# A decayed linear attention and a two-layer network on one core: the first layers of the last two token groups by seven products

## The chip, the core and the metric

The kernel runs on one core of a Trainium2 chip. A core has a matrix engine (TensorE, PE in the profile; its weight loads are listed as PEld), a vector engine (VectorE, DVE), a scalar engine for activation functions (ScalarE, ACT), a general engine (GpSimd, POOL) and a queue engine that issues transfers (SyncE, SP). Each works through its own list of instructions in order and waits for the others by semaphores. TensorE writes its sums to PSUM, eight banks of 128 rows by 512 float32 numbers; VectorE and ScalarE read and write PSUM and the main on-chip memory, SBUF.

The metric is the time of one execution on the device, in microseconds (us), as a median over runs. The profile is of one further execution; its span runs from the first to the last instruction.

## The reference

```python
# q, k, v: (4, 8, 768, 64)   lam: (8,)   w_in: (512, 2048)   w_out: (2048, 512)
for b in range(768 // 64):                       # blocks of 64 positions, each with a running state
    intra = (qb @ kb.T * Dmask) @ vb             # Dmask[i, j] = lam ** (i - j) for i >= j, else 0
    inter = (qb * lam_pow) @ kv_state            # lam ** (i + 1)
    out[:, :, sl] = intra + inter
    kv_state = lam ** 64 * kv_state + (kb * rev_pow).T @ vb
x = out.transpose(0, 2, 1, 3).reshape(3072, 512) # 8 heads of 64 side by side
h = x @ w_in
g = h * tanh(softplus(h))                        # Mish
return g @ w_out                                 # (3072, 512) float32
```

## The kernel before, in words

**Groups.** The 768 positions are cut into six groups (`NG`) of 128 (`C`); a group holds the 128 positions of all four batches, so 512 tokens (`GT`). For each group there are three kinds of work. Attention, batch by batch: `scores` (L238; matmuls into banks e and o, masked by DVE into `sb`), `outputs` (L259; matmuls into bank z, scaled by DVE into `xn`, turned by a transfer of SP into `xt`, the group's tokens in the layout for the first layer), `state` (L286; bank e, then DVE and POOL). The first layer: `x @ w_in` with Mish. The second layer: the product with `w_out`.

**The first layer, plain.** A *unit* (`unit`, L322) is 128 of the 2048 hidden columns for all 512 tokens: four matmuls of 512 columns into one bank and one Mish on ACT into `hsg`. Group `n + 1` has units 0 to 15. The banks A, B and C take turns (`next_bank`, L329). The weights `w_in` lie in four tiles `win[0]` to `win[3]` of 512 hidden columns each, so four units read one tile.

**The second layer by seven products.** `dense2` (L427) uses the Strassen-Winograd scheme: the product is cut into 2 x 2 blocks, and seven block products of sums take the place of eight. It works on banks G and H, in 14 *halves*: product 1, 2, 6, 5, 7, 3, 4, each for two blocks of tokens; a half is eight matmuls of 256 columns. Product 1 is copied from G to H by ACT (L440) before product 2 is added to G; product 5 goes by ACT to SBUF (`r5`, L447) and DVE makes `u4` from it and H (L449) before product 7 is added to H. The sums of hidden values that the products read are made by DVE (`token_sum`, L369), those of the weights once (`weight_sum`, L356).

**The order of the work.** It is written out by hand; each engine's list has the order of the program text. The loop at L701 runs n = 1 to 4. In iteration n, TensorE does the first layer of group n + 1 (units, `u`), the second layer of group n (halves, `h`), and for n up to 3 the attention of group m = n + 2 (`s_` for scores, `o_` for outputs). These are interleaved so that a half or a unit lies between an operation on another engine and the matmul that waits for it. At the end of iterations 1 to 3 the first two halves of group n + 1 are done. In iteration 4 there is no attention left. In iteration 3 it is that of the last group, which needs no `state`. After the loop `dense2_alone` (L479) does the second layer of the last group.

**Transfers.** POOL issues the loads of q, k and v, SP the transposes of k and q (`turn_dma`, L227), of `xn` and the stores. `kT` and `qT` have three buffers, each of two batches of a group.

Of the kernel before, what the change touches and what calls it, by code (L numbers as in the profile page):

```python
# [7 lines left out]
F32 = mybir.dt.float32  # L8
F16 = mybir.dt.float16
AF = mybir.ActivationFunctionType  # L10
ALU = mybir.AluOpType
# [9 lines left out]
def kernel(  # L21
# [10 lines left out]
    nc = tc.nc  # L32
    B, H, S, D = q.shape
    C = 128
    NG = S // C
    JP = H // 2
# [8 lines left out]
    WS = 4  # L45
# [43 lines left out]
    win = [const.tile([128, NKC, WQ], F16, name=f"win{s}") for s in range(WS)]  # L89
# [108 lines left out]
    xt, kT, qT, kd, sb, wst = {}, {}, {}, {}, {}, {}  # L198
# [7 lines left out]
    def flat(t, j):  # L206
        return t[:, 2 * j : 2 * j + 2, :].rearrange("p h c -> p (h c)")

    turned = {}

    def turn_pe(n, b, banks):

        srcs = (kn[n, b], qn[n, b])
        for src, name, to, tag in zip(srcs, ("kT", "qT"), (kT, qT), banks):
            pt = bank(tag, [JP, C], F16)
            for j in range(JP):
                nc.tensor.matmul(pt[:, j, :], flat(src, j), ident, is_transpose=True,
                                 start=(j == 0), stop=(j == JP - 1))
            if b % 2 == 0:
                turned[name, n] = work.tile([128, 2 * JP, C], F16, name=name, tag=name, bufs=3)  # L220
            to[n, b] = turned[name, n][:, b % 2 * JP : b % 2 * JP + JP, :]
            if name == "kT" or n > 0:
                nc.scalar.activation(to[n, b], pt, AF.Copy)
            else:
                nc.vector.tensor_copy(to[n, b], pt)

    def turn_dma(n, bp):  # L227
        for t, to in (("k", kT), ("q", qT)):
            tile_ = work.tile([128, 2 * JP, C], F16, name=f"{t}T", tag=f"{t}T", bufs=3)
            nc.sync.dma_start_transpose(out=tile_, in_=pairs[t, n, bp].rearrange("p h c -> p (h c)"))  # L230
            for i in range(2):
                to[n, 2 * bp + i] = tile_[:, i * JP : (i + 1) * JP, :]
# [113 lines left out]

    class Set:
        pass

    tsum = [const.tile([128, HK, HN], F16, name=f"tsum{i}") for i in range(4)]  # L350

    def w_quarter(r, c, s):

        return wout[2 * r + s][:, :, c * HN : (c + 1) * HN]

    def weight_sum(i, s):  # L356

        ks = slice(s * NKI // WS, (s + 1) * NKI // WS)
        a, b, op = (
            (w_quarter(0, 1, s), w_quarter(0, 0, s), ALU.subtract),  # L360
            (w_quarter(1, 1, s), tsum[0][:, ks, :], ALU.subtract),
            (w_quarter(1, 1, s), w_quarter(0, 1, s), ALU.subtract),
            (w_quarter(1, 0, s), tsum[1][:, ks, :], ALU.subtract),
        )[i]
        nc.vector.tensor_tensor(out=tsum[i][:, ks, :], in0=a, in1=b, op=op)
# [52 lines left out]
    def product(n, p, t, blk, fresh, lo=0, hi=HN):  # L418
        lhs, rhs = operands(n, p)
        for kk in range(HK):  # L420
            nc.tensor.matmul(t, lhs(kk, blk), rhs(kk)[:, lo:hi], start=(fresh and kk == 0),  # L421
                             stop=(kk == HK - 1), skip_group_check=True)

    def osum():
        return work.tile([128, 2, HN], F32, name="osum", tag="osum", bufs=3)
# [53 lines left out]
    def dense2_alone(n):  # L479

        x, z = bank("G", [2, HN]), bank("H", [2, HN])
        y = [(bank("A", [HN]), 0, 0, HN), (bank("B", [HN // 2]), 1, 0, HN // 2),
             (bank("C", [HN // 2]), 1, HN // 2, HN)]
        keep = lambda name: work.tile([128, 2, HN], F32, name=name, tag=name, bufs=1)

        def both(p, t, fresh):
            for blk in range(2):
                product(n, p, t[:, blk, :], blk, fresh and blk == 0)

        both(1, x, True)  # L490
# [10 lines left out]
        u3, u2 = keep("u3"), keep("u2")  # L501
# [12 lines left out]
        for t, blk, lo, hi in y:  # L514
            product(n, 3, t, blk, False, lo, hi)
        for t, blk, lo, hi in y:
            o = osum()
            nc.vector.tensor_tensor(out=o[:, blk, lo:hi], in0=t, in1=u2[:, blk, lo:hi], op=ALU.add)
            store(n, 0, 1, o[:, blk : blk + 1, lo:hi], blk, lo, hi)
# [48 lines left out]
    def sums(n, part, *which):  # L568
        for i in which:
            token_sum(n, i, part)  # L570
# [61 lines left out]
    later[3]()  # L632
    two_units(1, 12, 0)
    turn_dma(2, 1)

    def attend(n, b, kd_eng):
# [56 lines left out]
    def h(m=1):  # L693
        for _ in range(m):
            halves.pop(0)()
# [2 lines left out]

    for n in range(1, NG - 1):  # L701
        m = n + 2
        last = m >= NG - 1

        def u(*units):
            for ni in units:
                unit(n + 1, ni, next_bank())

        def s_(b):
            if m < NG:  # L710
                if not last:
                    decay_k(m, b, nc.vector)
                scores(m, b)

        def o_(b):
            if m < NG:
                outputs(m, b)
                if not last:
                    state(m, b, "e", nc.gpsimd)

        def fetch(*what):
            if m + 1 < NG:
                for t, bp in what:
                    load_pair(t, m + 1, bp)

        s_(0)
        if m < NG:
            turn_dma(m, 1)
        u(0)
        sums(n, 1, 0, 1)  # L730
        if n == 1:
            weight_sum(3, 0)
            weight_sum(3, 1)
        h(1)
        u(1)
        h(1)
        u(2)
        o_(0)
        fetch(("k", 0), ("q", 0))
        u(3)  # L740

        h(1)
        u(8)
        s_(1)
        sums(n, 1, 2, 3)
        h(1)
        u(9, 10)
        o_(1)
        fetch(("v", 0), ("k", 1))
        h(1)  # L750
        u(11)

        h(1)
        u(4)
        s_(2)
        if m + 1 < NG:
            turn_dma(m + 1, 0)
        u(5)
        h(1)
        u(6)  # L760
        o_(2)
        fetch(("q", 1), ("v", 1))
        h(1)
        sums(n + 1, 0, 0, 1)
        h(1)
        u(7)

        s_(3)
        h(1)
        u(12)  # L770
        h(1)
        o_(3)
        u(13)
        sums(n + 1, 0, 2, 3)
        h(1)
        u(14)
        if n + 1 < NG - 1:
            halves = dense2(n + 1)
            h(1)
        u(15)  # L780
        if n + 1 < NG - 1:
            h(1)

    sums(NG - 1, 1, 2, 0, 1, 3)
    dense2_alone(NG - 1)


# [28 lines left out]
```

## Time and profile before

| | |
|---|---|
| median of three runs | 213.22 us (211.72 to 213.25) |
| the profiled execution | 213.27 us |
| its span | 211.3 us |
| mean granted TensorE clock | 0.996 |
| iteration n = 3 of the loop | 140.45 to 170.06, 29.6 us |
| iteration n = 4 | 170.06 to 194.39, 24.3 us |
| `dense2_alone` and the last stores | 194.39 to 211.30, 16.9 us |

A row of the timeline gives start, duration, engine, line, operation and its tiles (written <- read), and in brackets the engine's idle time before it with what ended it. A matmul row's duration includes an end that overlaps the next matmuls, so the distance from one row's start to the next one's is what a block of matmuls takes of TensorE. The chain of waits lists these distances directly. DVE and ACT rows can overlap their neighbours in the same way.

### The profile page before, as it was taken

What the parts mean: (1) busy time and instruction counts of PE and PEld (TensorE: products, weight loads), DVE (VectorE), ACT (ScalarE), POOL (GpSimd) and SP (SyncE); (2) the same over time, 40 slices, a digit from 0 to 9 for tenths busy, and PEclk for the clock granted to TensorE, in tenths of its full rate; (3) what the DMA queues carried; (4) which work ended last, traced back from release to release, by engine and by line L of the source; (5) the groups of instructions that cost most, each with busy time, mean ns of one, the idle gap of its engine ahead of it and who ended that gap; (6) DMA issues with size and microseconds to landing.
All of it is one profiled execution on the core that took longest, in us unless ns stands there. A gap on an engine that the chain in (4) does not pass through costs nothing.

```text
span 211.3 us, 4221 instructions
## 1 busy us (share of the span) xinstructions
PE 201.0 (95%) x1757; PEld 135.0 (64%) x1757; DVE 124.5 (59%) x202; ACT 88.1 (42%) x152; POOL 77.6 (37%) x75
## 2 busy tenths in 40 slices
PE   7798999899999999999999999999999999999991
PEld 2366545688765456667666667766667765666891
DVE  6738749872875857647965657953638340153341
ACT  5354676658531124342254342254342454525300
POOL 7999554524565760653530763410000000000020
PEclk9999999999999999999999999999999999999998
DMA  8999999999939999799992499991112401013033
GB/s 128 140 162 206 159 179 158 187 207 174 127 75 129 214 158 170 156 139 128 177 250 74 55 153 135 169 248 55 21 28 74 119 8 50 0 50 102 0 102 99
DMA packets 109365, 26.23 MB, mean 124 GB/s; under 512 B 99490, under 2 KB 108834, under 8 KB 109346
## 3 DMA queue, kind: packets, MB, share of 16 engines
q0 software_dynamic: 77600, 13.37, 81.1%
q1 hardware_dynamic: 30704, 12.33, 28.0%
q10 hardware_dynamic: 1042, 0.26, 0.6%
q8 instruction: 14, 0.23, 0.4%
q14 instruction: 5, 0.04, 0.1%
HBM read 27.26 MB, written 6.29 MB: 159 GB/s over the span
## 4 chain that ended last, share of the span: by engine, by line
PE 85%; DVE 3%; DMA 3%; POOL 3%; ACT 2%; issue 2%; ACTq 0%; DVEq 0%
PE bG L421 15%; PE bH L421 13%; PE bB L314 11%; PE bC L314 11%; PE bA L314 11%; PE be L243 4%; PE bB L340 2%; PE bz L263 2%; PE bz L268 2%; DMA q<-in_q_dram 2%; PE bA L340 2%; PE bG L472 2%; PE bC L340 2%; PE bC L472 2%; POOL kd L236 1%
## 5 line engine op out<-in xcount | busy, mean ns | idle before, releaser
L314 PEld LDWEIGHTS <-win 128*128 128x128 f16 x328 | 30.4, 98 | 23.7 <-issue 0.3
L298 POOL TENSOR_TENSOR w<-raw,lbm 128x512 f16<-128x512 f32 x14 | 20.0, 1428 | 52.1 <-DVE raw L297 52.1
L421 PEld LDWEIGHTS <-gsum 128*128 128x128 f16 x336 | 30.9, 98 | 7.3
L247 DVE TENSOR_TENSOR sb<-be,dm 128x512 f16<-128x512 f32 x24 | 16.5, 687 | 22.6 <-PE bo L243 22.5
L421 PEld LDWEIGHTS <-hsg 128*128 128x128 f16 x240 | 23.4, 98 | 7.8
L314 PE MATMUL bA<-xt,win 128*128 128x512 f16 (+2 forms) x112 | 27.9, 372 | 0.2
L314 PE MATMUL bC<-xt,win 128*128 128x512 f16 x108 | 27.7, 379 | 0.0
L320 ACT ACTIVATE hsg<-bA 128x512 f16<-128x512 f32 x27 | 16.1, 597 | 26.1 <-PE bA L314 26.1
L314 PE MATMUL bB<-xt,win 128*128 128x512 f16 (+2 forms) x108 | 26.9, 371 | 0.0
L271 DVE TENSOR_TENSOR xn<-bz,lq 128x512 f16<-128x512 f32 x20 | 13.8, 690 | 19.8 <-PE bz L268 19.8
L320 ACT ACTIVATE hsg<-bB 128x512 f16<-128x512 f32 x26 | 15.5, 598 | 23.6 <-PE bB L314 23.6
L503 POOL TENSOR_TENSOR u<-u,u 128x512 f32<-128x512 f32 x1 | 1.3, 1273 | 64.2 <-DVE u L502 64.2
L320 ACT ACTIVATE hsg<-bC 128x512 f16<-128x512 f32 x27 | 16.2, 598 | 20.3 <-PE bC L314 20.2
L421 PE MATMUL bH<-tsum,gsum 128*128 128x256 f16 x160 | 20.4, 273 | 0.0
L421 PE MATMUL bG<-wout,hsg 128*128 128x256 f16 x160 | 20.2, 273 | 0.0
L384 DVE TENSOR_TENSOR gsum<-hsg 128x1024 f16<-128x1024 f16 x20 | 15.0, 752 | 6.4 <-ACT hsg L320 6.4
L247 DVE TENSOR_TENSOR sb<-bo,dm 128x512 f16<-128x512 f32 x24 | 16.3, 679 | 0.0
L340 PEld LDWEIGHTS <-win 128*128 128x128 f16 x128 | 12.1, 98 | 2.2 <-issue 0.6
L84 POOL DMA_DIRECT2D kn<-in_k_dram x10 | 12.0, 1199 | 2.8 <-PE be L289 1.6
L449 DVE TENSOR_TENSOR u<-bH,r 128x512 f32<-128x512 f32 x4 | 2.8, 690 | 17.3 <-ACT r L447 17.3
L84 POOL DMA_DIRECT2D qn<-in_q_dram x10 | 11.9, 1186 | 1.4 <-PE bz L263 0.7
L84 POOL DMA_DIRECT2D vn<-in_v_dram x10 | 11.9, 1187 | 0.3 <-issue 0.2
(119 smaller groups left out, 306.9 us busy)
## 6 DMA issues: line engine op xcount, KB each, us to landing
out_dram<-osum SPq DMA_DIRECT2D x23, 256.0 KB, 2.6
kn<-in_k_dram POOLq DMA_DIRECT2D x10, 256.0 KB, 8.8
qn<-in_q_dram POOLq DMA_DIRECT2D x10, 256.0 KB, 6.9
vn<-in_v_dram POOLq DMA_DIRECT2D x10, 256.0 KB, 8.3
wout<-in_moe_w_out_dram POOLq DMA_DIRECT2D x4, 512.0 KB, 15.2
win<-in_moe_w_in_dram POOLq DMA_DIRECT2D x3, 512.0 KB, 9.5
vz<-in_v_dram POOLq DMA_DIRECT2D x4, 128.0 KB, 4.5
kn<-in_k_dram POOLq DMA_DIRECT2D x3, 128.0 KB, 4.5
```

What stands on the lines that cost most here:

```text
L84: nc.gpsimd.dma_start(out=tile_, in_=rows(src, n, 2 * bp, 2))
L243: nc.tensor.matmul(p_[t][:, j, :], kT[n, b][rs, j, :], qT[n, b][rs, j, :], start=True, stop=True)
L247: nc.vector.tensor_tensor(out=sb[n, b, t], in0=p_[t], in1=dm[:, t], op=ALU.mult)
L263: nc.tensor.matmul(po[:, 2 * j : 2 * j + 2, :].rearrange("p h e -> p (h e)"), qT[n, b][:, j, :], wst[n, b][:, j, :], start=(j == 0), stop= ...
L271: nc.vector.tensor_tensor(out=xn, in0=po, in1=bc(lq, 2, D), op=ALU.mult)
L298: eng.tensor_tensor(out=w_new, in0=raw, in1=lbm, op=ALU.mult)
L314: nc.tensor.matmul(open_[n, ni][:, lo:hi], win[ni // 4][:, kc, (ni % 4) * 128 : (ni % 4) * 128 + 128], xt[n][:, kc, lo:hi], start=(opens a ...
L320: nc.scalar.activation(h_tile(n)[:, ni, :], open_.pop((n, ni)), AF.Mish)
L340: nc.tensor.matmul(t[:, u, :], win[ni // 4][:, kc, m : m + 128], xt[n][:, kc, cs], start=(u == 0 and kc == 0), stop=(kc == NKC - 1), skip_ ...
L384: nc.vector.tensor_tensor(out=gsum[n, i][:, ks, :], in0=a, in1=b, op=op)
L421: nc.tensor.matmul(t, lhs(kk, blk), rhs(kk)[:, lo:hi], start=(fresh and kk == 0), stop=(kk == HK - 1), skip_group_check=True)
L472: nc.tensor.matmul(po, hsg[n][:, ki, b * C : (b + 1) * C], wout[part][:, kk, :], start=(ki == 0), stop=(ki == NKI - 1))
```

## The change

Iterations 1 and 2 keep units; iterations 3 and 4 (first layers of groups 4 and 5) use *sets*. A set is one tile `win[s]`: 512 hidden columns for 512 tokens, cut into 2 x 2 blocks of hidden columns and tokens and 2 of the inner dimension. Seven products of four matmuls of 256 columns (`seven`) replace sixteen matmuls of 512 columns. The sets come in the order s = 0, 2, 1, 3.

One set runs as follows, with three banks a, b, c: product P1 into a; ACT copies a to b (`seed`); P2 is added to a, and ACT's Mish reads it. P5 goes into c and ACT copies it to SBUF (`p5`). P6 is added to b; DVE writes b + p5 into c. P7 is added to b; DVE writes b + p5 to SBUF (`c22`). P3 is added to c, then Mish. Mish of `c22`, P4 added to b, Mish of b. P4 and the last two Mish are *owed*: they come after the next set's P1, scores and seed (`settle`), so the seed of a set stands ahead of them on ACT. In iteration 3 the banks are A, B, C and, for every other set, A, C, B; in iteration 4 A, B, C and e, z, o.

The products read sums of tokens (`x_sums`: four DVE operations of 512 float16 elements per row, at the start of iterations 3 and 4) and sums of weights (`w_sum`: four per set, kept in `wsum`). The weight sums of the four sets are made on DVE in iterations 1 and 2, two places in each, behind the token sums of `s_(1)` and behind unit 5.

Besides: `kT` and `qT` have two buffers instead of three; the transposes of group m + 1, batches 0 and 1, are issued ahead of unit 4 and `s_(2)` instead of behind them; `dense2_alone` uses the tiles `p5` and `c22` for its `u3` and `u2`.

```diff
-                turned[name, n] = work.tile([128, 2 * JP, C], F16, name=name, tag=name, bufs=3)
+                turned[name, n] = work.tile([128, 2 * JP, C], F16, name=name, tag=name, bufs=2)
...
+    def w_sum(s, i, eng):
+        w, t = win[s], wsum[s]
+        a, b_, op = (
+            (w[:, 0:2, HC:], w[:, 2:4, HC:], ALU.add),
+            (t[:, 0], w[:, 0:2, 0:HC], ALU.subtract),
+            (w[:, 0:2, 0:HC], w[:, 0:2, HC:], ALU.subtract),
+            (w[:, 2:4, 0:HC], t[:, 1], ALU.subtract),
+        )[i]
+        eng.tensor_tensor(out=t[:, i], in0=a, in1=b_, op=op)
...
+    def x_sums(n):
+        x = xt[n]
+        t = [work.tile([128, 2, HC], F16, name=f"xsum{i}", tag=f"xsum{i}", bufs=1) for i in range(4)]
+        xsum[n] = t
+        for i, (a, b_) in enumerate((
+            (x[:, 0:2, HC:], x[:, 0:2, 0:HC]),
+            (x[:, 2:4, HC:], t[0]),
+            (x[:, 2:4, HC:], x[:, 0:2, HC:]),
+            (x[:, 2:4, 0:HC], t[1]),
+        )):
+            nc.vector.tensor_tensor(out=t[i], in0=a, in1=b_, op=ALU.subtract)
...
+    def seven(o, i, t, fresh):
+        w, x, ws, xs = win[o.s], xt[o.n], wsum[o.s], xsum.get(o.n)
+        for u in range(2):
+            for kk in range(2):
+                us = slice(u * 128, u * 128 + 128)
+                lhs, rhs = (
+                    lambda: (w[:, kk, us], x[:, kk, 0:HC]),
+                    lambda: (w[:, 2 + kk, us], x[:, 2 + kk, 0:HC]),
+                    lambda: (ws[:, 3, kk, us], x[:, 2 + kk, HC:]),
+                    lambda: (w[:, 2 + kk, HC + u * 128 : HC + u * 128 + 128], xs[3][:, kk, :]),
+                    lambda: (ws[:, 0, kk, us], xs[0][:, kk, :]),
+                    lambda: (ws[:, 1, kk, us], xs[1][:, kk, :]),
+                    lambda: (ws[:, 2, kk, us], xs[2][:, kk, :]),
+                )[i - 1]()
+                nc.tensor.matmul(t[:, u, :], lhs, rhs, start=(fresh and u == 0 and kk == 0),
+                                 stop=(kk == 1), skip_group_check=True)
...
+    def set_step(o, step):
+        if step == "m1":
+            o.a = bank(o.banks[0], [2, HC])
+            seven(o, 1, o.a, True)
+        elif step == "seed":
+            o.b = bank(o.banks[1], [2, HC])
+            nc.scalar.activation(o.b, o.a, AF.Copy)
+        elif step == "m2":
+            seven(o, 2, o.a, False)
+            mish(o, 0, 0, o.a)
+        elif step == "m5":
+            o.c = bank(o.banks[2], [2, HC])
+            seven(o, 5, o.c, True)
+            o.p5 = work.tile([128, 2, HC], F32, name="p5", tag="p5", bufs=1)
+            nc.scalar.activation(o.p5, o.c, AF.Copy)
+        elif step == "m6":
+            seven(o, 6, o.b, False)
+            nc.vector.tensor_tensor(out=o.c, in0=o.b, in1=o.p5, op=ALU.add)
+        elif step == "m7":
+            seven(o, 7, o.b, False)
+            o.c22 = work.tile([128, 2, HC], F32, name="c22", tag="c22", bufs=1)
+            nc.vector.tensor_tensor(out=o.c22, in0=o.b, in1=o.p5, op=ALU.add)
+        elif step == "m3":
+            seven(o, 3, o.c, False)
+            mish(o, 0, 1, o.c)
+        elif step == "m4":
+            mish(o, 1, 1, o.c22)
+            seven(o, 4, o.b, False)
+            mish(o, 1, 0, o.b)
...
+    KINDS = {1: "pppp", 2: "pppp", 3: "ssss", 4: "ssss"}
+    WSUMS = {(1, 0): (0,), (1, 1): (2,), (2, 0): (1,), (2, 1): (3,)}
...
+        for i, x in enumerate((0, 2, 1, 3)):
+            alone = (("A", "B", "C"), ("e", "z", "o")) if m >= NG else (("A", "B", "C"), ("A", "C", "B"))
+            turn = i % 2 if kinds[i - 1] == "s" else 0
+            sets.append(set_of(n + 1, x, alone[turn]) if kinds[i] == "s" else None)
+        owed = []
...
+        def settle():
+            while owed:
+                mm(owed.pop(), "m4")
+        def opening(i):
+            if kinds[i] == "s":
+                mm(i, "m1")
+                s_(i)
+                mm(i, "seed")
+                settle()
+            elif i == 0:
+                s_(i)
+        def closing(i):
+            mm(i, "m7", "m3")
+            owed.append(i)
...
+        opening(0)
         if m < NG:
             turn_dma(m, 1)
+        if "s" in kinds:
+            x_sums(n + 1)
+        if kinds[0] == "s":
+            h(1)
+            mm(0, "m2", "m5")
+            sums(n, 1, 0, 1)
+            h(1)
+            mm(0, "m6")
+            o_(0)
+            fetch(("k", 0), ("q", 0))
+            closing(0)
...
+        opening(1)
         h(1)
+        if kinds[1] == "s":
+            mm(1, "m2", "m5")
+            sums(n, 1, 2, 3)
+            h(1)
+            mm(1, "m6")
+            o_(1)
+            fetch(("v", 0), ("k", 1))
+            h(1)
+            closing(1)
...
+        opening(2)
         h(1)
         if m + 1 < NG:
             turn_dma(m + 1, 0)
+        if kinds[2] == "s":
+            mm(2, "m2", "m5", "m6")
+            o_(2)
+            fetch(("q", 1), ("v", 1))
+            h(1)
+            closing(2)
+            h(1)
+            sums(n + 1, 0, 0, 1)
+            h(1)
...
+        opening(3)
+        if kinds[3] == "s":
+            h(1)
+            mm(3, "m2", "m5")
+            h(1)
+            mm(3, "m6")
+            o_(3)
+            h(1)
+            mm(3, "m7", "m3")
+            owed.append(3)
+            sums(n + 1, 0, 2, 3)
...
+        more = n + 1 < NG - 1
+        if more:
             halves = dense2(n + 1)
             h(1)
+        settle()
+        if kinds[3] != "s":
+            u(15)
+        if more:
             h(1)
```

More of the change, by code (lines that the diff above doesn't have):

```diff
@@ new lines, in set_of @@
+    def set_of(n, s, banks):
+        o = Set()
+        o.n, o.s, o.banks = n, s, banks
+        return o
+    def seven(o, i, t, fresh):
[14 more added lines that the diff above has]
+                                 stop=(kk == 1), skip_group_check=True)
@@ L500, in dense2_alone @@
         both(6, z, False)
-        u3, u2 = keep("u3"), keep("u2")
+        u3, u2 = keep("p5"), keep("c22")
         nc.vector.tensor_tensor(out=u3, in0=z, in1=p1, op=ALU.add)
@@ L724, in fetch, with ws @@
                     load_pair(t, m + 1, bp)
-        s_(0)
+        def ws(n, i):
+            for x in WSUMS.get((n, i), ()):
+                for t in range(4):
+                    w_sum(x, t, nc.vector)
+        kinds = KINDS[n]
+        sets = []
+        for i, x in enumerate((0, 2, 1, 3)):
+            alone = (("A", "B", "C"), ("e", "z", "o")) if m >= NG else (("A", "B", "C"), ("A", "C", "B"))
+            turn = i % 2 if kinds[i - 1] == "s" else 0
+            sets.append(set_of(n + 1, x, alone[turn]) if kinds[i] == "s" else None)
@@ new lines, with mm @@
+        owed = []
+        def mm(i, *steps):
+            for x in steps:
+                set_step(sets[i], x)
+        def settle():
[12 more added lines that the diff above has]
+            owed.append(i)
@@ L754 @@
-        u(4)
-        s_(2)
+        if "s" in kinds:
[9 more added lines that the diff above has]
+            closing(0)
+        else:
+            u(0)
+            sums(n, 1, 0, 1)
+            if n == 1:
+                weight_sum(3, 0)
+                weight_sum(3, 1)
+            h(1)
+            u(1)
+            h(1)
+            u(2)
+            o_(0)
+            fetch(("k", 0), ("q", 0))
+            u(3)
@@ new lines @@
+        opening(1)
+        h(1)
+        if kinds[1] == "s":
[7 more added lines that the diff above has]
+            closing(1)
+        else:
+            u(8)
+            settle()
+            s_(1)
+            sums(n, 1, 2, 3)
+            ws(n, 0)
+            h(1)
+            u(9, 10)
+            o_(1)
+            fetch(("v", 0), ("k", 1))
+            h(1)
+            u(11)
@@ L756 @@
+        opening(2)
+        h(1)
         if m + 1 < NG:
             turn_dma(m + 1, 0)
[L758 to L777, printed above, removed]
+        if kinds[2] == "s":
[6 more added lines that the diff above has]
+            sums(n + 1, 0, 0, 1)
+            h(1)
+        else:
+            u(4)
+            settle()
+            s_(2)
+            u(5)
+            ws(n, 1)
+            h(1)
+            u(6)
+            o_(2)
+            fetch(("q", 1), ("v", 1))
+            h(1)
+            sums(n + 1, 0, 0, 1)
+            h(1)
+            u(7)
@@ new lines @@
+        opening(3)
+        if kinds[3] == "s":
+            h(1)
+            mm(3, "m2", "m5")
+            h(1)
+            mm(3, "m6")
+            o_(3)
+            h(1)
+            mm(3, "m7", "m3")
+            owed.append(3)
+            sums(n + 1, 0, 2, 3)
+        else:
+            s_(3)
+            h(1)
+            u(12)
+            settle()
+            h(1)
+            o_(3)
+            u(13)
+            sums(n + 1, 0, 2, 3)
+            h(1)
+            u(14)
+        more = n + 1 < NG - 1
```

31 lines of the change are left out of this document (7 added, 24 removed).

## The prediction

> **What bounds the kernel now.** I read the page's busy shares and its chain first, then the windows of the two iterations that get the new products, then the order of time on each engine there.
>
> ```profile
> PE 201.0 (95%) x1757; PEld 135.0 (64%) x1757; DVE 124.5 (59%) x202; ACT 88.1 (42%) x152; POOL 77.6 (37%) x75
> PEclk9999999999999999999999999999999999999998
> PE 85%; DVE 3%; DMA 3%; POOL 3%; ACT 2%; issue 2%; ACTq 0%; DVEq 0%
> ```
>
> TensorE carries the chain, at full clock. The next rows are two stretches: the length, then the busy time of PE, PEld, DVE, ACT, POOL. The first is iteration n=3 (output halves of group 3, first layer of group 4, attention of group 5), the second n=4 (no attention).
>
> ```profile
> 140.45:170.06 29.61, 29.61 (x258) 19.71 (x257) 14.81 (x24) 11.93 (x20) 0.00 (x0) 1.00 0.26 67
> 170.06:194.39 24.33, 24.33 (x163) 15.66 (x161) 7.71 (x12) 11.33 (x19) 0.00 (x0) 1.00 0.10 34
> ```
>
> PE is busy in every part of both, while DVE and ACT have half their time free: only PE's work and PE's waits count here. The chain prices that work:
>
> ```profile
> 172.00 0.86 PE bA L314 x4
> 172.86 0.87 PE bG L421 x8
> ```
>
> A unit (four matmuls of 512 columns) is 0.865 us; a half (eight of 256) is 0.872, so 0.109 a matmul and 0.436 for a block of four. Check: n=4 has 16 units and 12 halves, 13.84 + 10.46 = 24.30 of 24.33; n=3 has two halves more (1.74) and four batches of attention in the other 3.54, 0.885 each.
>
> **The products.** Per set 16 matmuls of 512 (3.46) become 28 of 256 (3.05): 0.41 less, over eight sets 3.27 us less. That is the whole gain. The iterations without waits would be 29.55 - 1.63 = 27.92 and 24.30 - 1.63 = 22.67. Their loads of 28 weights a set lie under the matmuls as those of the halves do.
>
> **The new loops.** A set's products share banks with ACT and DVE, so PE now waits for round trips. How long is one?
>
> ```profile
> 169.19 1.04 PE L421 MATMUL bG<-wout,hsg 128*128 128x256 f16 x8
> 170.33 0.58 ACT L440 ACTIVATE bH<-bG 128x512 f32<-128x512 f32 x1 [0.34 <-PE bG L421]
> 170.96 1.03 PE L421 MATMUL bG<-wout,hsg 128*128 128x256 f16 x8
> ...
> 186.58 1.04 PE L421 MATMUL bG<-wout,gsum 128*128 128x256 f16 x8
> 186.78 0.69 DVE L452 TENSOR_TENSOR osum<-bH,r 128x512 f32<-128x512 f32 x1 [3.02 <-PE bH L421]
> ...
> 6.56 0.41 DVE L225 COPY qT<-bz 128x512 f16<-128x512 f16 x1
> 7.03 0.26 PE L243 MATMUL be<-qT,kT 64*128 64x128 f16 x1 [0.34 <-DVE qT L225]
> ```
>
> Through ACT: the half issued from 169.19 has used its slot at 170.06; the copy runs 170.33 to 170.91 and the next product on G starts at 170.96: 0.90. Through DVE: the slot of H ends where G's begins, 186.58; DVE starts 0.20 later, takes 0.69, and PE follows 0.06 after a DVE end (6.97 to 7.03): 0.95. DVE's sum into a bank isn't in this trace; I take 0.69 from the same form into SBUF. Each wait is then the round trip less what PE has to do meanwhile.
>
> In n=4, where nothing of attention is left to lie between:
> - p2 of the halves adds to G, which the copy to H reads. Before, unit 0 covered it; now block P1 alone: 0.90 - 0.44 = 0.46.
> - Set 0, P7 directly behind P6 on one bank, with `c = b + p5` to read between: 0.95.
> - Sets 1 and 3, one half between P6 and P7: 0.95 - 0.87 = 0.08 each.
> - P4 waits for `c22`, which reads P7's sum. Sets 0 and 1 have P3 and the next P1 between (0.87): 0.08 each. Set 3 has P3 alone: 0.51.
> - Set 2: ACT is the queue. Its rows at their closest:
>
> ```profile
> 36.36 0.60 ACT L223 ACTIVATE kT<-bH 128x512 f16<-128x512 f16 x1
> 36.84 0.62 ACT L223 ACTIVATE qT<-bz 128x512 f16<-128x512 f16 x1
> ```
>
> 0.48 apart. From the end of set 1's P3 ACT has Mish, the seed, two Mish, the r5 copy (L447), Mish, the p5 copy; the first starts at 0.2, so r5 ends near 2.75 and p5 near 3.7. PE reaches the half of product 7, which needs DVE's u4 behind r5 (2.75 + 0.69 + 0.1 = 3.5), at 3.1 (P1, P4 with its 0.08, a half, P2, P5, P6): 0.4. It reaches P7 at 4.4, and `c` behind p5 is read at 4.5: 0.1.
>
> Together 2.74; n=4 becomes 22.67 + 2.74 = 25.4, 1.1 longer than now.
>
> In n=3 the scores and outputs lie between, but DVE's queue is longer.
>
> ```profile
> 161.78 1.05 PE L421 MATMUL bG<-wout,gsum 128*128 128x256 f16 x8
> 161.88 0.69 DVE L247 TENSOR_TENSOR sb<-be,dm 128x512 f16<-128x512 f32 x1
> 162.49 0.68 DVE L247 TENSOR_TENSOR sb<-bo,dm 128x512 f16<-128x512 f32 x1
> ...
> 164.40 0.39 PE L263 MATMUL bz<-w,qT 128*128 128x128 f16 x4
> 164.86 1.03 PE L314 MATMUL bC<-xt,win 128*128 128x512 f16 x4
> ...
> 170.02 0.69 DVE L384 TENSOR_TENSOR gsum<-hsg 128x1024 f16<-128x1024 f16 x1 [3.08 <-ACT hsg L320]
> 170.75 0.69 DVE L384 TENSOR_TENSOR gsum<-gsum,hsg 128x1024 f16<-128x1024 f16 x1
> 171.36 0.69 DVE L384 TENSOR_TENSOR gsum<-hsg 128x1024 f16<-128x1024 f16 x1
> ...
> 206.12 0.42 DVE L518 TENSOR_TENSOR osum<-bA,u 128x256 f32<-128x256 f32 x1 [0.34 <-PE bA L421]
> 206.46 0.28 DVE L518 TENSOR_TENSOR osum<-bB,u 128x128 f32<-128x128 f32 x1
> ...
> 102.21 0.68 DVE L236 TENSOR_TENSOR kd<-kn,lk 128x512 f16<-128x512 f16 x1
> ```
>
> Outputs take 0.46 of PE, scores the other 0.43 of a batch. `sb` starts 0.10 after the scores' slot; DVE's pitch is 0.61, or 0.73 where an operation reads the one before. `x_sums` (512 elements of f16) isn't in the trace. Between 0.28 (128 f32) and 0.68 (`kd`, 512 f16 with a broadcast f32 factor) I take 0.42: 1024 f16 cost what 512 f32 cost, so 512 f16 should cost what 256 f32 do, 0.34 apart.
>
> From the start of n=3: P1 to 0.44, scores to 0.86, the half from 0.90 (0.04 of wait for G), P2 from 1.77 to 2.21. DVE: `sb` 0.96 and 1.57, first x sum 2.17 to 2.59. P5 needs it: 2.65, a wait of 0.44. P5, a half, P6, outputs run to 4.86. DVE meanwhile: x sums to 3.62, token sums to 4.95, then `c` to 5.64, so P7 starts at 5.70: 0.84. Sets 1 to 3 have a half between P6 and P7 or between P4 and the next need, and no wait over 0.1 by the same walk. Sum 1.32: n=3 becomes 27.92 + 1.32 = 29.2, 0.3 shorter.
>
> **Weight sums in n=1 and n=2**, four on DVE at two places of each.
>
> ```profile
> 96.46 0.68 DVE L247 TENSOR_TENSOR sb<-bo,dm 128x512 f16<-128x512 f32 x1
> 98.38 0.69 DVE L271 TENSOR_TENSOR xn<-bz,lq 128x512 f16<-128x512 f32 x1 [1.24 <-PE bz L268]
> ...
> 100.18 1.39 DVE L384 TENSOR_TENSOR gsum<-hsg 128x1024 f16<-128x1024 f16 x1
> ...
> 103.42 0.68 DVE L247 TENSOR_TENSOR sb<-bo,dm 128x512 f16<-128x512 f32 x1
> ...
> 104.28 0.40 PE L268 MATMUL bz<-vn,sb 128*128 128x64 f16 x8
> ```
>
> The second place falls into the idle 1.24 ahead of `xn`; behind it DVE runs without a gap to `sb` of batch 3, which ends at 104.10, 0.18 before PE uses it. Four sums at 0.34 with one dependence are 1.45: a shift of 0.1 to 0.2, so about 0.05 of wait. At 0.61 apart (2.55) it would be 1.1 per iteration; nothing excludes zero either. I take 0.1 for both iterations, with bounds 0 and 2.2. The first place is followed by `xn` and then by free time on DVE, with the next scores seven blocks away: nothing.
>
> **What costs nothing.** The transposes of the next group move ahead of unit 4 and the scores of batch 2 on SP, and their tiles have one buffer fewer:
>
> ```profile
> 118.33 1.21 POOL L84 DMA_DIRECT2D kn<-in_k_dram  x1
> ...
> 123.70 1.27 SPq L230 DMA_TRANSPOSE kT<-kn  x1
> ...
> 165.78 1.19 SPq L274 DMA_TRANSPOSE xt<-xn  x1
> DMA to landing us min/median/max: 2.4/2.4/5.1
> ```
>
> The transpose already starts 5.4 us after its load's issue, when PE has just finished batch 1's outputs, the last reader of the slot it would now share; its own reader is the next iteration. SP is held for the load either way, and only `xn` of batch 2 queues behind. Without this cover a wait at the iteration's start would cost up to a transpose. The last `xt` transpose of n=3 was issued 4.3 us before n=4 (170.06); now `xn` stands behind set 3's `c`, and by the walk 2.9 are left. Its landing takes 2.4, and P1 reads only the other half of the tokens; at the longest, 5.1, the x sums would come 2.2 late and P5 0.5. POOL's queue is unchanged; the tail after n=4 has the same products, and its first two (3.5) cover the last Mish.
>
> **Sum.** 213.27 (the profiled execution, 0.05 over the median) - 3.27 + 2.74 + 1.32 + 0.1 = 214.2; as a median 214.1.
>
> **The clock, and a rule against the change.** PE gets about ten pauses of up to 0.9 us.
>
> ```profile
> 8.00:12.00 4.00, 2.97 (x25) 1.91 (x24) 2.67 (x7) 2.18 (x5) 4.00 (x6) 1.00 2.31 147
> ...
> 10.93 0.28 PE L243 MATMUL be<-qT,kT 64*128 64x128 f16 x1 [1.03 <-ACT kT L223]
> ```
>
> With a pause of 1.03 and PE busy 2.97 of 4.00 the granted clock stayed 1.00, so I add nothing. The Trainium skill, "TensorE: Matmul & The Clock Gate", section "A second HAM failure mode: psum-queue depth-cycling", says that short pauses between groups of matmuls cycling through PSUM banks can make the clock swing between half and full. By that rule the sum would rise as in the rival below; the trace so far speaks against it.
>
> **Rivals.**
> - *The waits are half hidden* (chance 0.08): round trips on ACT and DVE overlap more than I walked. 213.27 - 3.27 + 2.1 = 212.1, and 211 or less if most go. For it: DVE and ACT are half idle. Against: three of the largest (0.95, 0.51, 0.46) are on one bank with nothing between, and idle engines don't shorten them.
> - *DVE's f16 sums are as slow as `kd`* (chance 0.14), 0.61 apart instead of 0.34. Then the weight sums cost 2.2, and in n=3 the x sums delay P5 by 0.26 and P7 by 1.1 in all: 214.1 + 2.1 + 1.1 = 217.3. It passes 1% from about 0.45 apart. For it: `kd` itself, and 1.39 for a token sum that met POOL. Against: the scaling from 0.69 to 0.42 to 0.28, and POOL idle in n=3 and n=4.
> - *The clock swings* (chance 0.02): with set 0 of n=4 (3.05 of matmuls, pauses on both sides of it) at half clock, 214.1 + 3.1 = 217.2.
> - That fewer than 28 matmuls a set are issued, or another order, the written program order excludes.
>
> **Numbers.** The forecast keeps 0.76. 80% needs its own bounds. Down: x sums at the cheap end (0.28), which takes 0.6 off n=3, no price for the weight sums (0.1), and 0.2 less at each of the five large waits: 212.4. Up: half of the slow-sum case (1.6) and a landing between its two ends (0.3): 216.0. One per cent is 2.1 us, about what this kernel's runs (211.72 to 213.25) can tell from no change. Faster by that needs the half-hidden case in full, 0.08; slower is the slow sums and the clock, 0.16; within, 0.76.
>
> **What would show it.** Right: first-layer rows of 256 columns in blocks of 0.44; PE idle about 2.7 in n=4, the longest piece near 0.8 to 0.95 ahead of set 0's P7 with DVE's sum as releaser; in n=3 one wait for an x sum and one for `c`; n=3 near 29.2, n=4 near 25.4. Wrong: PE idle under 1.5 in both together, x sums 0.6 apart, PE waiting for `sb` in n=1 or n=2, or a granted clock under 1.

## The result, and the profile after

The changed kernel takes 214.65 us at the median of 19 runs (212.99 to 215.11), the kernel before 213.14 in 19 runs beside them (211.65 to 213.78). The ratio is 1.0079, with an interval of 1.0059 to 1.0100: slower, by about 0.8 per cent. (This ratio is an estimate over all the runs beside each other, and so are those below; the quotient of the two medians is 1.0071.) The forecast was 214.1.

The page after, its busy shares and its clock row:

```profile
span 212.9 us, 4496 instructions
PE 199.3 (94%) x1853; PEld 144.3 (68%) x1853; DVE 142.1 (67%) x242; ACT 94.7 (45%) x168; POOL 77.7 (36%) x75
PEclk9999999999999999999999999999999999999999
```

TensorE (PE) has 96 matmuls more, each of the new ones half as wide, and is busy 1.7 us less; the span is 1.6 longer (212.9 against 211.3). So PE waits about 3.3 more. Where, the stretches of n=3 and n=4 show (length, busy time of PE, PEld, DVE, ACT, POOL, then granted clock, DMA share, GB/s):

```profile
140.50:169.84 29.34, 28.37 (x306) 24.35 (x304) 21.28 (x35) 15.47 (x28) 0.00 (x0) 1.00 0.27 67
169.84:195.51 25.67, 23.89 (x211) 20.27 (x208) 13.42 (x22) 14.15 (x27) 0.00 (x0) 1.00 0.13 45
```

n=3 is 0.27 shorter than before (29.61), n=4 is 1.34 longer (24.33), and from 195.51 to the end are about 17.4 in place of 16.9. In these rows PE's busy time still holds short waits: a block of four matmuls takes a slot of 0.436, but its row shows 0.60, so a wait up to 0.16 lies under the row's end. Waits below are therefore counted by distance from one start to the next. The two places in n=3:

```profile
143.14 0.60 PE L395 MATMUL bC<-xsum,wsum 128*128 128x256 f16 x4 [0.27 <-DVE xsum L374]
...
146.21 0.60 PE L395 MATMUL bB<-xsum,wsum 128*128 128x256 f16 x4 [0.70 <-DVE bC L420]
```

The first is P5 behind the first x sum: P2's slot ended at 142.71, a wait of 0.43. The second is set 0's P7 behind `c`, which VectorE (DVE) writes: 0.87. In n=4 the four largest waits, with the matmul row ahead of each and the DVE row that makes the first P7's wait:

```profile
169.84 0.60 PE L395 MATMUL bA<-xt,win 128*128 128x256 f16 x4
170.73 1.03 PE L506 MATMUL bG<-wout,hsg 128*128 128x256 f16 x8 [0.29 <-ACT bH L525]
...
173.35 0.60 PE L395 MATMUL bB<-xsum,wsum 128*128 128x256 f16 x4
174.81 0.60 PE L395 MATMUL bB<-xsum,wsum 128*128 128x256 f16 x4 [0.86 <-DVE bC L420]
...
184.26 0.60 PE L395 MATMUL bB<-xsum,wsum 128*128 128x256 f16 x4
185.15 1.03 PE L506 MATMUL bH<-tsum,gsum 128*128 128x256 f16 x8 [0.28 <-DVE u L534]
...
194.13 0.60 PE L395 MATMUL bo<-xt,wsum 128*128 128x256 f16 x4
195.08 0.60 PE L395 MATMUL bz<-xsum,win 128*128 128x256 f16 x4 [0.34 <-DVE c L424]
```

```profile
174.06 0.70 DVE L420 TENSOR_TENSOR bC<-bB,p 128x512 f32<-128x512 f32 x1 [1.08 <-PE bB L395]
```

By distance they are 0.45 (G behind the copy to H), 1.02 (P7: from 173.79, where P6's slot ends, to 174.81), 0.45 (product 7 behind `u4`) and 0.51 (P4 behind `c22`). With five small ones (0.07 to 0.16), 3.00 in n=4.

### The profile page after: what moved, and what is told of

It is laid out like the page before. It is cut to its first block, busy times and chain, and to the rows that moved or that the text cites. A ratio compares the mean times of both kernels' runs of the same rounds, so it can differ in the third digit from the quotient of the medians.

```text
span 212.9 us, 4496 instructions
## 1 busy us (share of the span) xinstructions
PE 199.3 (94%) x1853; PEld 144.3 (68%) x1853; DVE 142.1 (67%) x242; ACT 94.7 (45%) x168; POOL 77.7 (36%) x75
## 4 chain that ended last, share of the span: by engine, by line
PE 80%; DVE 6%; ACT 4%; DMA 3%; POOL 3%; issue 2%; ACTq 0%; DVEq 0%
PE bG L506 14%; PE bH L506 12%; PE bA L314 6%; PE bC L314 6%; PE bB L314 6%; PE be L243 3%; PE bB L395 3%; PE bC L395 3%; PE bB L340 2%; PE bz L263 2%; PE bz L268 2%; DMA q<-in_q_dram 2%; PE bA L340 2%; PE bG L557 2%; PE bC L340 2%
## 5 line engine op out<-in xcount | busy, mean ns | idle before, releaser
L314 PEld LDWEIGHTS <-win 128*128 128x128 f16 x200 | 18.2, 98 | 14.2 <-issue 0.3
L588 POOL TENSOR_TENSOR c<-p,u 128x512 f32<-128x512 f32 x1 | 1.3, 1273 | 65.2 <-DVE p L587 65.2
L314 PE MATMUL bA<-xt,win 128*128 128x512 f16 (+2 forms) x72 | 17.7, 368 | 0.2
L320 ACT ACTIVATE hsg<-bA 128x512 f16<-128x512 f32 x17 | 10.2, 597 | 15.6 <-PE bA L314 15.6
L314 PE MATMUL bC<-xt,win 128*128 128x512 f16 x64 | 16.5, 380 | 0.0
L314 PE MATMUL bB<-xt,win 128*128 128x512 f16 (+2 forms) x64 | 15.6, 366 | 0.0
L320 ACT ACTIVATE hsg<-bB 128x512 f16<-128x512 f32 x15 | 9.0, 598 | 14.6 <-PE bB L314 14.6
L395 PEld LDWEIGHTS <-wsum 128*128 128x128 f16 x128 | 12.5, 97 | 4.1 <-issue 2.6
L320 ACT ACTIVATE hsg<-bC 128x512 f16<-128x512 f32 x16 | 9.6, 599 | 11.2 <-PE bC L314 11.1
L340 PEld LDWEIGHTS <-win 128*128 128x128 f16 x128 | 12.1, 98 | 2.2 <-issue 0.6
```

The costliest lines, as they stand in the source:

```text
L314: nc.tensor.matmul(open_[n, ni][:, lo:hi], win[ni // 4][:, kc, (ni % 4) * 128 : (ni % 4) * 128 + 128], xt[n][:, kc, lo:hi], start=(opens a ...
L320: nc.scalar.activation(h_tile(n)[:, ni, :], open_.pop((n, ni)), AF.Mish)
L340: nc.tensor.matmul(t[:, u, :], win[ni // 4][:, kc, m : m + 128], xt[n][:, kc, cs], start=(u == 0 and kc == 0), stop=(kc == NKC - 1), skip_ ...
L395: nc.tensor.matmul(t[:, u, :], lhs, rhs, start=(fresh and u == 0 and kk == 0), stop=(kk == 1), skip_group_check=True)
```

## The experiments

The theory was that of the prediction: PE's work falls by 3.27, and each microsecond given back is a wait of PE with a named operation of another engine ahead of it. Its rivals: the new loops cost something that lies in no single wait (a lower clock, busier engines, the longer program), or the other parts of the change cost the time.

### Which part costs what

Three kernels undo parts of the change. `e3_rest` keeps weight sums, two buffers and the earlier transposes, but issues no set:

```diff
-    KINDS = {1: "pppp", 2: "pppp", 3: "ssss", 4: "ssss"}
+    KINDS = {1: "pppp", 2: "pppp", 3: "pppp", 4: "pppp"}
```

> No sets at all: the weight sums of iterations 1 and 2, two buffers and the moved transposes alone. Theory: at most 0.1 us, ratio 0.998 to 1.002, no new wait of PE, the last stretch as before (16.9). Rival (weight sums delay DVE's sb and so PE): ratio 1.003 or more, PE waiting for sb in iterations 1 and 2.

Measured 213.3 at the median, ratio 0.9999 (0.9971 to 1.0028). These parts cost nothing that can be measured, within about 0.6 us to either side.

`e1_only3` has sets in n=3 alone, `e2_only4` in n=4 alone:

```diff
# e1_only3
+    KINDS = {1: "pppp", 2: "pppp", 3: "ssss", 4: "pppp"}
# e2_only4
+    KINDS = {1: "pppp", 2: "pppp", 3: "pppp", 4: "ssss"}
```

> Sets only in iteration 3 (group 4); iteration 4 keeps units. Theory (gain of the products less PE's waits on ACT and DVE): iteration 3 near 29.3 us as in the changed kernel (29.6 before), iteration 4 back at 24.3, so 0.2 us less than the kernel before, ratio 0.997 to 1.001. Rival (what is common to both iterations costs: weight sums, buffers, moved transposes): ratio 1.003 or more with iteration 4 at 24.3.

> Sets only in iteration 4 (group 5). Theory: iteration 4 near 25.7 us (24.3 before), iteration 3 at 29.6, ratio 1.005 to 1.009, the larger value if the last stretch is again 0.5 us longer. Rival (the loss comes from the queues of iteration 3 or from the common parts): ratio within 0.002 of 1.

`e1_only3` took 212.47, ratio 0.9982 (0.9956 to 1.0009); `e2_only4` 213.66, ratio 1.0040 (1.0014 to 1.0067), a little less than I had expected (1.005 to 1.009). Their stretches of n=3 and n=4, `e1_only3` first:

```profile
139.95:169.29 29.34, 28.36 (x306) 24.30 (x303) 21.82 (x36) 15.48 (x28) 0.00 (x0) 1.00 0.28 71
169.29:193.86 24.57, 24.45 (x162) 15.67 (x161) 7.14 (x12) 11.28 (x19) 0.00 (x0) 1.00 0.13 44
```

```profile
139.55:169.17 29.62, 29.62 (x259) 19.72 (x258) 16.36 (x28) 11.93 (x20) 0.00 (x0) 1.00 0.29 76
169.17:194.84 25.67, 23.89 (x210) 20.28 (x208) 11.96 (x18) 14.17 (x27) 0.00 (x0) 1.00 0.11 35
```

Each iteration with sets has the length that it has in the changed kernel (29.34 and 25.67), whether or not the other has them too. The net loss lies in n=4 alone. Two oddities of 0.24 are left. In `e1_only3` the first unit of n=4 starts 0.28 late behind the last set, at 169.57; in `e3_rest` n=3 takes 29.85 (the table below), because its first unit starts 0.25 late, at 141.24, while `e2_only4`, with the same n=3, has 29.62. The profile names no releaser at either place. But a unit reads all 512 tokens of `xt`, and in these two the last transpose of `xt` ahead of the unit landed late: issued at 166.49 it took 2.9, to about 169.4, and issued at 136.06 it took 5.1, to about 141.2. In `e2_only4` it had landed at about 139.8, ahead of the unit at 139.98. So these landings are the likely cause; no run tests it.

### Moving work under the waits

If the waits are all, then the same 28 matmuls a set, in another order, must win. `e4_cover4` writes n=4 so that a half lies between P6 and P7 of every set and between the copy of G and its next use, and puts the last P4 behind the first product of the closing stage:

```diff
+            for i in range(4):
+                mm(i, "m1", "seed")
+                if i == 0:
+                    x_sums(n + 1)
+                h(1)
+                settle()
+                mm(i, "m5")
+                if i < 2:
+                    sums(n, 1, 2 * i, 2 * i + 1)
+                h(1)
+                if i == 2:
+                    sums(n + 1, 0, 0, 1)
+                mm(i, "m2", "m6")
+                h(1)
+                closing(i)
...
-        settle()
+        if more and kinds[3] == "s":
+            h(1)
+            settle()
...
+    def between():
+        settle()
+        sums(NG - 1, 1, 2, 0, 1, 3)
...
+    dense2_alone(NG - 1, between)
```

> The changed kernel with the same products, but in iteration 4 every set has a half ahead of P4 of the set before, one between P5 and P2 and one between P6 and P7; the second half of the next group's product 1 goes ahead of set 3's P4 at the end of iteration 3, and the last P4 behind product 1 of the last stretch. Theory (the waits are the loss): PE's waits from the start of iteration 4 fall from 3.0 to about 0.85 us, 2.1 us less than the changed kernel, ratio to the kernel before 0.995 to 0.999. Rival (the blocks themselves, their weight loads or the added load on ACT and DVE are the loss): ratio stays at 1.004 or more, with PE busy without pauses and blocks longer than 0.44.

A miss: 213.59, ratio 1.0041 (1.0012 to 1.0069). Set 0's P7 now waited 0.15 and the last P4 not at all, but set 2's P7 had taken their place. PE's row and DVE's queue ahead of it:

```profile
187.72 0.60 PE L395 MATMUL bB<-xsum,wsum 128*128 128x256 f16 x4 [0.97 <-DVE bC L420]
```

```profile
185.65 0.68 DVE L469 TENSOR_TENSOR gsum<-hsg 128x1024 f16<-128x1024 f16 x1
186.36 0.69 DVE L469 TENSOR_TENSOR gsum<-gsum,hsg 128x1024 f16<-128x1024 f16 x1
186.97 0.69 DVE L420 TENSOR_TENSOR bC<-bB,p 128x512 f32<-128x512 f32 x1
```

My own order had put two token sums of the next group ahead of `c` in DVE's list, and with an `osum` before them `c` started 1 us late, at 186.97: the half between P6 and P7 was long done, and P7 waited 1.14. `e8_cover4b` corrects that, and the order of two operations on ScalarE (ACT):

```diff
-                h(1)
-                if i == 2:
+                if i == 3:
                     sums(n + 1, 0, 0, 1)
+                h(1)
...
-        elif step == "m4":
+        elif step == "e4":
             mish(o, 1, 1, o.c22)
+            o.early = True
+        elif step == "m4":
+            if not getattr(o, "early", False):
+                mish(o, 1, 1, o.c22)
...
+            mm(3, "e4")
             h(1)
             settle()
```

> The order of e4, with two things corrected: the token sums that stood ahead of c in VectorE's queue in set 2 go behind product 5 of set 3, and the first half of c22's Mish of set 3 is issued ahead of the second half of the closing at the end of n=3. Theory (every added microsecond is a wait of TensorE with a named piece of another engine ahead of it): set 2's P7 waits 0.15 in place of 1.14, G about 0.05 in place of 0.24, the waits of n=4 sum to about 0.85, so 1.2 less than e4's 213.59: 212.4, ratio to the kernel before 0.9965 (0.994 to 0.999). Rival (the token sums are late only because VectorE is behind by then in any order): another P7 waits 1 us in place of set 2's, ratio 1.004 as in e4. The 0.40 before VectorE's last operation stays in both.

211.92, ratio 0.9966 (0.9943 to 0.9990), as the theory had it; the kernel before had a median of 212.41 beside it. `e5_cover34` does the same for n=3, for the two waits seen there:

```diff
+        if "s" in kinds:
+            x_sums(n + 1)
         opening(0)
...
-        if "s" in kinds:
-            x_sums(n + 1)
...
             mm(0, "m6")
             o_(0)
             fetch(("k", 0), ("q", 0))
+            h(1)
             closing(0)
...
             mm(1, "m2", "m5")
             sums(n, 1, 2, 3)
-            h(1)
             mm(1, "m6")
```

> As e8, and in n=3 three pieces of work moved: the x sums ahead of the scores of batch 0, a half of the dense products between P6 and P7 of set 0, and none between P5 and P6 of set 1. Theory: the waits of n=3 (0.04, 0.43 and 0.87 in the changed kernel) come to about 0.1, n=3 takes 28.1 in place of 29.3; with e8's n=4 the kernel takes 211.2, ratio 0.991 (0.988 to 0.994), so faster than the kernel before, by about 1.9 of the 3.27 that the products save. Rival (VectorE's queue is the bound in n=3: the x sums, moved ahead, push the scores' own work back): n=3 stays at 29.3 and the ratio at e8's.

209.90 in five runs, ratio 0.9879 (0.9854 to 0.9905): faster than both kernels, and just under the range that I had expected. Its stretches:

```profile
139.03:167.07 28.04, 28.04 (x307) 24.33 (x304) 21.38 (x35) 14.94 (x28) 0.00 (x0) 1.00 0.27 67
167.07:190.50 23.43, 23.43 (x211) 20.30 (x209) 12.83 (x22) 14.46 (x27) 0.00 (x0) 1.00 0.14 46
```

n=3 is at 28.04 where the prediction's sum without waits is 27.92, n=4 at 23.43 where it is 22.67 (the last P4's slot of 0.44, now behind the first closing product, is counted in). Against the kernel before, the two gain 1.57 + 0.90 = 2.47. The tail gives about 0.6 back (below), so 1.9 of the 2.5 us between the medians (209.90 and 212.41) lie in these parts. The rest need not be the order's doing: in the profiles the stretch ahead of n=3 ended at 139.03 here and at 140.45 before, though in it `e5_cover34` does what `e8_cover4b` (139.72) and the changed kernel (140.50) do. So 0.9% can be put down to the order, and not the whole 1.2%.

### One wait at a time

`e6_half` takes the changed kernel and moves one half in n=4 from behind set 2 to between P6 and P7 of set 0:

```diff
             mm(0, "m6")
...
+            if m >= NG:
+                h(1)
             closing(0)
...
             closing(2)
-            h(1)
+            if m < NG:
+                h(1)
```

> The changed kernel with one half of the dense products in n=4 moved from behind set 2 to between P6 and P7 of set 0. Theory (P7 waits 1.02 because nothing stands between it and the copy of bank B's sum by VectorE): that wait goes to about 0.15, the halves behind come one place earlier and their own waits (0.45 and 0.11) may shift by 0.1 or so; 0.7 to 0.9 less than the changed kernel, ratio to the kernel before about 1.004 (1.002 to 1.007). Rival (the wait comes out later, since the piece moved is lacking behind set 2): set 2's place takes up 0.5 to 1.0 and the ratio stays 1.008.

213.03, ratio 1.0047 (1.0019 to 1.0076). The ratio is as expected, the stretch is not: P7's wait fell from 1.02 to 0.16, but n=4 from 25.67 only to 25.21. The rest was taken back elsewhere than I had said, at set 1's P4:

```profile
181.23 0.60 PE L395 MATMUL bz<-xsum,win 128*128 128x256 f16 x4 [0.55 <-DVE c L424]
```

```profile
178.46 0.70 DVE L420 TENSOR_TENSOR bo<-bz,p 128x512 f32<-128x512 f32 x1 [2.61 <-PE bz L395]
179.89 0.69 DVE L534 TENSOR_TENSOR u<-bH,r 128x512 f32<-128x512 f32 x1 [0.73 <-ACT r L532]
180.50 0.68 DVE L424 TENSOR_TENSOR c<-bz,p 128x512 f32<-128x512 f32 x1
```

All halves come one place earlier, and so `u4`, which itself waits for ACT's copy `r5`, stands ahead of `c22` (here `c`) in DVE's list: P4 waits 0.71 in place of 0.07. `u4`'s own wait of 0.45 is gone, set 2's P7 has 0.33 in place of 0.11. The sum, -0.86 + 0.64 - 0.45 + 0.22 = -0.45, is what n=4 lost (0.46).

`e7_tail` moves only the last P4 with its Mish and the last token sums behind the first product of the closing stage:

```diff
-        settle()
+        if more:
+            settle()
...
-    sums(NG - 1, 1, 2, 0, 1, 3)
-    dense2_alone(NG - 1)
+    def between():
+        settle()
+        sums(NG - 1, 1, 2, 0, 1, 3)
+
+    dense2_alone(NG - 1, between)
```

> The changed kernel with the last set's P4, its Mish and the last token sums put behind the first product of the closing stage. Theory: P4's wait of 0.51 behind c goes, nothing of the closing stage waits for it at once, ratio about 1.0055 (1.003 to 1.008). Rival (the last token sums, issued later, hold up the last group's sums at the end): the end moves back by as much and the ratio stays 1.008 or grows.

214.11 in five runs, ratio 1.0076 (1.0047 to 1.0105), which holds both answers. The trace decides: n=4, with the P4's slot counted in, went from 25.67 to 25.17, and no wait for `c` is left there; the tail was 17.5 in place of 17.4.

### All stretches side by side

Worked out from the windows of each profile, in us; the tail runs from the end of n=4 to the end of the span. In e4, e5, e7 and e8, where the last P4 lies behind the first closing product, its 0.44 is counted in n=4.

| kernel | n=3 begins | n=3 | n=4 | tail | ratio |
|---|---|---|---|---|---|
| before | 140.45 | 29.61 | 24.33 | 16.9 | 1 |
| changed | 140.50 | 29.34 | 25.67 | 17.4 | 1.0079 |
| e3_rest | 140.56 | 29.85 | 24.32 | 16.9 | 0.9999 |
| e1_only3 | 139.95 | 29.34 | 24.57 | 16.7 | 0.9982 |
| e2_only4 | 139.55 | 29.62 | 25.67 | 16.8 | 1.0040 |
| e4_cover4 | 140.71 | 29.35 | 24.79 | 17.3 | 1.0041 |
| e6_half | 139.00 | 29.35 | 25.21 | 17.2 | 1.0047 |
| e7_tail | 139.18 | 29.34 | 25.17 | 17.5 | 1.0076 |
| e8_cover4b | 139.72 | 29.34 | 23.43 | 17.3 | 0.9966 |
| e5_cover34 | 139.03 | 28.04 | 23.43 | 17.5 | 0.9879 |

### The tail

The tail of the changed kernel is about 0.48 longer (spans are given to 0.1), which no step of the prediction had. The distances of its matmuls are as before: from the end of n=4 to DVE's sum of the second last product it takes 10.70 in both (195.51 to 206.21, and 194.39 to 205.09). What differs stands at the end of the chain of waits (start, length, what), first before, then after:

```profile
205.81 2.29 DMA out_dram<-osum
...
208.13 0.05 DVEq L518
208.18 0.04 issue
208.22 0.29 DVE osum L518
```

```profile
206.93 2.15 DMA out_dram<-osum
...
209.16 0.40 issue
209.56 0.29 DVE osum L603
```

Between the landing of the store that it waits for and the last DVE operation lie 0.48 (209.08 to 209.56) instead of 0.12 (208.10 to 208.22). Of this, 0.40 instead of 0.04 is listed as issue, time in which the engine waited for nothing that the profile shows. The same 0.40 stands in e4 to e8; e1, e2 and e3 have 0.04. All kernels with 0.40 have 242 instructions on DVE in the page, those with 0.04 have 202 to 230. Is it the length of DVE's program? `e9_pad` is `e3_rest` with 24 instructions more on DVE and the same work:

```diff
+        if n == NG - 2 and part == 1 and ws_ is None:
+            for j in range(4):
+                token_sum(n, i, part, (4 + j, 5 + j))
+            return
+        if n == NG - 1 and part == 0 and ws_ is None:
+            for j in range(4):
+                token_sum(n, i, part, (j, j + 1))
+            return
```

> e3 with eight token sums of the last two groups (second part of group 4's, first part of group 5's) each cut into four instructions of a quarter of the width: the same work, 24 instructions more on VectorE, 242 as in the changed kernel in place of 218. VectorE's last operation, the final osum, starts 0.04 behind the landing that it waits for in the kernel before, e1, e2 and e3 (202 to 230 instructions) and 0.40 behind it in every kernel with 240 or more. Theory A (it goes by how long VectorE's program is): 0.40 behind the landing here too, the tail 0.36 longer than e3's. Theory B (it goes by the order of the seven products in both groups): 0.04, as in e3. It is a look at one profile; the time is not what is asked.

```profile
PE 199.1 (95%) x1757; PEld 134.0 (64%) x1757; DVE 131.7 (63%) x242; ACT 88.1 (42%) x152; POOL 77.7 (37%) x75
...
207.46 0.04 issue
207.51 0.29 DVE osum L612
```

242 instructions, and 0.04: the number of DVE's instructions alone doesn't make it. (One run, 212.62 beside 211.58 of the kernel before.) What the six kernels with 0.40 have in common is that both groups are made by sets, and with that 4496 instructions in all, 1853 on PE and 168 on ACT, where the others have at most 4370, 1805 and 160; no run separates these. The profile also lists small transfers of two queues named "instruction". The last one of 0.02 MB on the first (q8) falls 2 to 8 us ahead of DVE's last operation in the kernels with 0.04, and 11 to 12 us ahead in those with 0.40 (in the changed kernel between 197 and 198). On the second (q14) a transfer of 0.01 MB falls 0.5 to 0.75 us behind the start of that operation in all six with 0.40, and in none of the others within 3 us of it; in `e9_pad` these transfers lie where they lie in `e3_rest`. So the gap goes with the place of these transfers in all eleven profiles; no run shows whether one causes the other. The cause stays open.

## Why the prediction was right

**The gain.** Blocks of 256 columns lie 0.436 apart, as taken. `e5_cover34` reaches n=3 within 0.12 of the sum without waits, and nearly all of its 0.76 over the sum in n=4 are five waits of 0.12 to 0.16. The 3.27 are real, and the added weight loads cost nothing. (The terms of the prediction's check of n=3 add up to 29.58, and it went on from 29.55; the 0.03 change nothing.)

**The waits.** By the prediction's own steps:

| step | predicted | measured |
|---|---|---|
| n=4: p2 on G behind the copy to H | 0.46 | 0.45 |
| n=4: set 0, P7 behind `c` | 0.95 | 1.02 |
| n=4: sets 1 and 3, P7 | 0.08 each | 0.15, 0.16 |
| n=4: P4 of sets 0 and 1 behind `c22` | 0.08 each | 0.08, 0.07 |
| n=4: set 2, the half behind `u4`, then P7 | 0.4, 0.1 | 0.45, 0.11 |
| n=4: set 3's P4 | 0.51 | 0.51 |
| n=3: P5 behind the first x sum | 0.44 | 0.43 |
| n=3: set 0's P7 behind `c` | 0.84 | 0.87 |
| sum with G in n=3 (0.04) | 4.06 | 4.34 |

The walk through the queues held almost to the hundredth: P5 was to start 2.65 into n=3 and started at 2.64, P7 at 5.70 and started at 5.71. The one term that was a little small is the round trip through DVE. I had taken 0.20 from the end of PE's slot to DVE's start, 0.69 and 0.06; in set 0 of n=4 it was 0.27 (173.79 to 174.06), 0.70 and 0.05, 1.02 in all, and the 0.07 come back in the P7 of sets 1 and 3. That makes n=4 25.67 in place of 25.4; n=3 came to 29.34 against 29.2.

**The x sums and weight sums**, the widest unknown. The second and third of the x sums:

```profile
143.12 0.42 DVE L374 TENSOR_TENSOR xsum<-xt,xsum 128x512 f16<-128x512 f16 x1
143.46 0.42 DVE L374 TENSOR_TENSOR xsum<-xt 128x512 f16<-128x512 f16 x1
```

0.42 each and 0.34 apart, the value taken; the rival with 0.61 apart falls. In n=1 the four weight sums of the second place took 1.46 of DVE (97.11 to 98.57) for a forecast of 1.45, and `xn` came at 98.57 in place of 98.38. TensorE paid nothing for it: its rows are 0.05 later than in the kernel before at the first unit of n=1, ahead of any weight sum (79.92 for 79.87), and still 0.05 behind this place (104.11 for 104.06) and at the start of n=3 (140.50 for 140.45). So the term of 0.1 came to nothing, the lower of its bounds. `e3_rest` agrees, though its interval is too wide to tell 0.1 from nothing.

**What costs nothing.** The last `xt` transpose of n=3 was issued at 167.04, 2.80 ahead of n=4 (2.9 by the prediction's walk), but it took 3.0 to land and not 2.4, and the first x sum of n=4 waited for it:

```profile
170.10 0.43 DVE L374 TENSOR_TENSOR xsum<-xt 128x512 f16<-128x512 f16 x1 [0.78 <-DMA xt<-xn]
```

P5 of that set did not wait all the same: it starts at 172.04, where P2's slot ends.

**The clock.** With a dozen pauses of up to 1.02 in n=3 and n=4 the granted clock is 1.00 in both stretches. The rival from the Trainium skill ("TensorE: Matmul & The Clock Gate", section "A second HAM failure mode: psum-queue depth-cycling"), by which such pauses can make the clock swing, did not come about in any of the profiles of these iterations shown here.

**Waits half hidden.** That rival falls for the order of the changed kernel: every large wait stood in full. (Of the three waits that the prediction sets against it only P7's has nothing between; the 0.46 and 0.51 are what a block between leaves over.) It was right in another sense, as e5 shows: engines half idle can hide most of it, once the order on PE leaves something to do. What n=3 and n=4 take over the sum without waits fell from 4.42 to 0.88.

**What failed.** By the medians the change cost 1.5 where 0.9 was forecast. The largest miss is the tail. "The tail after n=4 has the same products": it has, but the step took its length as unchanged too, and it grew by about 0.48. Of this 0.36 is the gap ahead of DVE's last operation, less 0.14 of a shorter landing (2.15 for 2.29), and 0.2 to 0.3 lies behind that operation up to the end. The cause is open. n=3 fell by 0.27 for a forecast of 0.31, and n=4 grew by 1.34 for a forecast of 1.11. These three would give 0.75 more than predicted; 0.05 less ahead of n=3, and about 0.22 less outside the span (1.75 against 1.97), bring it to 0.48: 214.65 against 214.16 for the profiled execution. The part outside the span is in no step of the prediction, so that much of the closeness is luck.

## What to carry to other kernels

Fewer matmul columns are worth only what the order leaves: price each new dependence as a round trip less the work that stands between on TensorE, and put that work there before the edit, not after. The same products lost 0.8% in one order and won about 0.9% in another. An operation moved to cover one wait is also moved in every other engine's list, so walk those lists again: two misses here (e4's token sums, e6's `u4`) were an early operation standing ahead of an urgent one.

## What the runs showed of the hardware that was not expected

- A round trip PE to DVE to PE on one bank of PSUM took 1.02 us with nothing between: 0.27 to start, 0.70 for 128 x 512 float32, 0.05 back.
- Before its last operation DVE stood 0.40 us with nothing to wait for that the profile shows in all six profiles where both groups are made by sets, 0.04 in the other five; its count of instructions alone does not set it (242 with 0.04 in `e9_pad`).
- The time at which n=3 begins differs by up to 1.7 us between profiles (139.00 to 140.71), also among kernels that have the same program up to there. A comparison of a change in n=3 or n=4 by single runs would drown in that; the lengths of like stretches nearly all repeat to 0.01.
